# A gated linear-recurrence layer and its feed-forward block: the last block's sums and stores in two halves, and the clamps of the gate logits moved ahead in the schedule

## The chip, the core and the metric

The kernel runs on one core of a Trainium2 chip. The core has a matrix engine (PE, which also loads its weights: PEld), a vector engine (DVE), a scalar engine (ACT, which evaluates functions by tables), a general engine (POOL) and a sequencer for transfers (SP). Each engine takes its own instructions strictly in order and waits for the others through semaphores. DMA transfers are issued by SP or by ACT and run beside the engines. The metric is the device time of one execution in microseconds; lower is better.

## The reference

Two stages. The first keeps a 48x48 state for each of 4x8 heads over 768 steps; the second is a feed-forward block with an unusual activation.

```python
f = 1.0 / (1.0 + np.exp(-f_logit))                      # q, k, v, f_logit: (4, 8, 768, 48)
for t in range(S):
    state = f[:, :, t, :, None] * state + np.einsum('bhd,bhe->bhde', k[:, :, t], v[:, :, t])
    y[:, :, t] = np.einsum('bhd,bhde->bhe', q[:, :, t], state)
x = y.transpose(0, 2, 1, 3).reshape(3072, 384)
h = x @ w_in                                            # (384, 2048)
g = h * erf(np.maximum(h, 0.0) + np.log1p(np.exp(-np.abs(h))))
out = g @ w_out                                         # (2048, 384)
```

## The kernel before

The 3072 rows of `x` are cut into 24 chunks of 128 rows, two to a block: 12 blocks of 256 rows. A chunk `g` passes through four stages. `stage_d` (L374) multiplies the prepared gate logits by a triangle on PE (L380), and ACT and DVE make decayed copies of q and k from it (L383, L386, L395, L399). `stage_t` (L403) transposes them on PE and copies the results from PSUM: `qA` by two ACT instructions (L418), `kT` by ACT or, from chunk 9, by DVE (L422). `stage_s` (L443) makes the scores and updates the state (DVE L438, L439); `stage_y` (L504) makes `y` on PE (L525), and ACT copies it into `xT` (L529). The PSUM tiles of `stage_d`, `stage_t` and `stage_y` come in turn from one pool of two buffers, `ps_at`, so `stage_y` has to wait until `stage_t`'s copies have freed one.

Before `stage_d`, `prepare` (L357) turns a whole block's logits into log(1+exp(-x)): a clamp on DVE (L360, 128x768 elements, in place), then Exp and Ln on ACT (L364, L365, in place), with a table load ahead of them if ACT last used the other set of functions (L347).

The second stage per block: `hidden` (L578) makes four groups of 1024 columns on PE (L587), each copied by ACT from PSUM (L594). `activate` (L539) then works on a group in steps: Exp on ACT (L157), two Tanh on ACT (L160), two multiplications on DVE (L165), Tanh on ACT (L559), a last multiplication on DVE (L561); two groups overlap, so that one step of one group's L561 goes with the next group's second L165. `project_first` (L659, blocks 0 and 1) is the plain product with `w_out`; `project` (L687, blocks 2 to 11) uses seven half-size products instead of eight, whose factors come from sums on DVE (L615). Its parts are added up by DVE in `plus` (L726) into five row pieces `rows_sb` (a slice of the tile `scratch`), and `store` (L652) sends four of them to the output in one transfer on SP (384 KB, L654).

The order of the work is written by hand. Iteration `it` walks through a list of slots, each a step of the second stage (`slots`, L761: a slot of `hidden` is one product of 128x256, of `project` one of 128x192; the profile counts two matmul instructions for each, as the data are 32-bit). After a slot `s` the loop (L930 to L985) puts in, in this order: rounding steps of the weights, a stage of the recurrence if `s` is in the list `at`, loads of logits, `prepare` of block `it + 3` at `prepare_at` (14 slots ahead of the `stage_d` that needs it, L928), an activation step (`act_step`, in iteration 2 where `s % 5` is 1 or 3), and a step of sums. All engines' queues follow from this one order. In iteration 2 the stages stand at slots 3, 11, 19, 28 (d9, s8, t9, y8 for chunks 9 and 8) and on, and `prepare_at` is 22.

In the last block `project` computes products 1, 2, 6, then 5, 7, then 3 and 4 in turn; 3 and 4 share a PSUM tile of pool `ps_sc`. After the last product DVE does one sum of two pieces (128x384) and one of a single piece (128x192), then SP stores all 256 rows. What follows in every engine's program is a conditional jump: the kernel holds a second, general version for extreme gates (`general`, L991), and `flag` (L1168, L1169) says whether it is needed. Each engine loads the flag, jumps over the general code and signs off; SP waits for every DMA's semaphore first.

Of the kernel before, what the change touches and what calls it, by code (L numbers as in the profile page):

```python
# [43 lines left out]
FP32 = mybir.dt.float32  # L44
# [26 lines left out]
P = 128  # L71
# [3 lines left out]
def kernel(  # L75
# [10 lines left out]
    nc = tc.nc  # L86
# [10 lines left out]
    CPB = 2  # L97
    TB = CPB * P
    n_blocks = B * S // TB
# [118 lines left out]
    lts = {}  # L218
# [124 lines left out]
    def use_exp_ln():  # L343
        if sets[0] == EXP_LN:
            return
        sets[0] = EXP_LN
        nc.scalar.add_instruction(  # L347
            mybir.InstLoadActFuncSet(
                act_func_set_id=EXP_LN, name=nc.get_next_instruction_name(),
                engine=mybir.EngineType.Activation, ins=[], outs=[],  # L350
            )
        )
# [1 line left out]
    def other_set():  # L354
        sets[0] = 0

    def prepare(blk, j0, j1):  # L357

        lt = lts[blk][:, j0:j1, :].rearrange("t j c -> t (j c)")
        nc.vector.tensor_scalar(  # L360
            out=lt, in0=lt, scalar1=LOGIT_MIN, scalar2=None, op0=ALU.max
        )
        use_exp_ln()
        nc.scalar.activation(out=lt, in_=lt, func=AF.Exp, scale=-1.0)  # L364
        nc.scalar.activation(out=lt, in_=lt, func=AF.Ln, bias=1.0)  # L365

    busy = []

# [283 lines left out]
    def store(blk):  # L652
# [3 lines left out]
            in_=rows_sb[:, 0:4, :].rearrange("p (t two) c -> p t (two c)", t=CPB),  # L656
        )

    def project_first(blk):  # L659

        ops = ps_moe.tile([P, 2, 512], FP32, name="ops", tag="moe")
        for gi in range(n_g):
            gr = groups[blk, gi]
            for tt in range(CPB):
                for j in range(FG):
                    ft = gi * FG + j
                    assert n_pieces + ft * n_pieces // n_ft in rounded
                    while not gr["done"]:
                        act_step()
                    nc.tensor.matmul(  # L670
                        ops[:, tt, 0:d_model],
                        lhsT=gr["h"][:, j, tt * P : (tt + 1) * P],
                        rhs=w_out_sb[:, ft, :],
                        start=(ft == 0), stop=(ft == n_ft - 1),
                    )
                    if j == FG - 1 and tt == CPB - 1:
                        if blk == 0:
                            to_sum.append(sum_w(gi))
                        if gi == n_g - 1:
                            nc.scalar.copy(  # L680
                                out=rows_sb[:, 0:4, :].rearrange("p (t two) c -> p t (two c)", t=CPB),
                                in_=ops[:, :, 0:d_model],
                            )
                            store(blk)
                    yield

    def project(blk):  # L687


        ops = [ps_moe.tile([P, 2, 512], FP32, name="ops", tag="moe") for _ in range(2)]  # L690
        end = blk == n_blocks - 1
        ops.append(ps_sc.tile([P, 2, 512], FP32, name="ops", tag="sc") if end else ops[1])
        place = {n: ops[i][:, j, k * DH : (k + 1) * DH] for n, (i, j, k) in {
            1: (0, 0, 0), 2: (0, 1, 0), 6: (0, 1, 1), 5: (1, 0, 0), 7: (1, 0, 1), 3: (2, 1, 0), 4: (2, 1, 1),
        }.items()}
        first = [1, 2, 5, 3]

        def pair(n):
            i, j = {2: (0, 1), 5: (1, 0), 3: (2, 1)}[n]
            return ops[i][:, j, 0 : 2 * DH].rearrange("p (n c) -> p n c", n=2)  # L700

        def products(gis, ns):
            for gi in gis:
                gr = groups[blk, gi]
                while gr["sums"] is None:
                    sum_step()
                a11, a12, a21, a22 = blocks(gr["h"])
                w = w_out_sb[:, FG * gi : FG * (gi + 1), :]
                s, t = gr["sums"], w_sums(gi)
                for j in range(2):  # L710
                    w1, w2 = w[:, j, :], w[:, 2 + j, :]
                    for n in ns:
                        x, y = {
                            1: (a11, w1[:, 0:DH]), 2: (a12, w2[:, 0:DH]), 3: (s[2], w2[:, DH:]),
                            4: (a22, t[:, 3, j, :]), 5: (s[0], t[:, 0, j, :]),
                            6: (s[1], t[:, 1, j, :]), 7: (a21, t[:, 2, j, :]),
                        }[n]
                        nc.tensor.matmul(  # L718
                            place[n], lhsT=x[:, j, :], rhs=y,
                            start=(gi == 0 and j == 0 and n in first),  # L720
                            stop=(gi == n_g - 1 and j == 1), skip_group_check=True,
                        )
                        yield

        def plus(out, x, y):
            nc.vector.tensor_tensor(out=out, in0=x, in1=y, op=ALU.add)  # L726

        o = rows_sb
        yield from products((0, 1), (1, 2, 6))
        yield from products((0,), (5, 7, 3, 4))  # L730
        to_sum.appendleft(sum_h(groups[blk, 3]))
        yield from products((1,), (5, 7, 3, 4))
        yield from products((2, 3), (1, 2, 6))
        nc.scalar.copy(out=o[:, 3, :], in_=place[1])  # L734

        plus(o[:, 0:5:4, :], o[:, 3:4, :].broadcast_to((P, 2, DH)), pair(2))
        def fives():

            plus(o[:, 3:5, :], o[:, 4:5, :].broadcast_to((P, 2, DH)), pair(5))

        yield from products((2, 3), (5, 7))
        if end:

            fives()
        yield from products((2, 3), (3, 4))
        if not end:
            fives()
        plus(o[:, 1:3, :], o[:, 3:5, :], pair(3))
        plus(o[:, 3, :], o[:, 3, :], place[7])
        store(blk)  # L750
# [42 lines left out]
    with tc.manual_schedule():  # L793
# [119 lines left out]
        for it in range(n_blocks):  # L913
# [16 lines left out]
            for s, _ in enumerate(gen):  # L930
                due += (1 if s < 42 else 0.6 if s < 72 else 0.3) if it == 0 else 0.42 if it == 1 else 0.6
                while due >= 1:
                    weights_step()
                    due -= 1
                if s % 6 == 3:
                    load_more()
                if at and s == at[0]:
                    at.popleft()
                    f, g = todo.popleft()
                    f(g)  # L940
                    if f in (stage_y, stage_y_s):
                        if g + NSV < n_chunks:
                            load_sv(g + NSV)
                        load_to(g + LOOK)
                        if g == 2:
                            load(5, "v")
                            load_piece(7)
                if it == 0 and s == 14:
                    prepare(2, 0, CPB)
                if it == 0 and s == 9:  # L950
                    load_f(6)
                    load_f(7)
                if s == n // 2 and it + 4 < n_blocks:
                    for j in range(CPB):
                        load_f((it + 4) * CPB + j)
                if it + 3 < n_blocks and s == prepare_at:
                    prepare(it + 3, 0, CPB)
                if it < 2:
                    step = it == 1 and s % 6 == 3
                elif it == 2:  # L960
                    step = s % 5 in (1, 3)
                elif it == 3:
                    step = s % 7 in (1, 4)
                elif it == n_blocks - 1:
                    step = s % 3 == 1
                else:
                    step = s % 9 in (2, 6)
                if step:
                    act_step()
                if it == 2:  # L970
                    if s % 2:
                        sum_step()
                elif it > 2:
                    if s == n - n_h and it < n_blocks - 1:
                        to_sum.extend(sum_h(groups[it - 1, gi]) for gi in range(NS))
                    if it == n_blocks - 1 and s % n_o == 40 and s < 2 * n_o:
                        blk = n_blocks - 2 + s // n_o
                        to_sum.extend(sum_h(groups[blk, gi]) for gi in range(NS))
                    if it == 3:
                        if s % 2:  # L980
                            sum_step()
                    elif s < n_o or s % 3 == 0 or it == n_blocks - 1:
                        sum_step()
                if it == n_blocks - 2 and s in (5, 40):
                    next(check)  # L985
# [215 lines left out]
```

## Time and profile before

| what | value |
|---|---|
| median of 6 runs | 619.54 us (618.51 to 621.52) |
| profiled execution, its own time | 619.03 us |
| its span, first to last instruction | 617.3 us |
| mean granted PE clock | 0.981 |
| busy: PE / PEld | 588.4 us (95%) / 515.0 us (83%) |
| busy: DVE / ACT / POOL | 460.3 us (75%) / 382.4 us (62%) / 15.4 us (2%) |
| clamp on DVE (L360, 128x768), x10 of 14 | 0.55 us median |
| Exp and Ln on ACT (L364, L365) | 0.84 us each, median |
| ACT's waits for the clamp (L364 for L360) | 16.0 us in 8 waits, longest 5.0 |
| store of a block (384 KB), issue to landing, x12 | 2.4 / 2.6 / 4.5 us (min / median / max) |

The span leaves out 1.7 us of the profiled execution's own time. Busy shares are means over phases with different limits: PE is close to saturated from about 80 us on, while the weights are still being rounded on DVE and ACT in the first quarter.

### The profile page before, as it was taken

The page shows a single profiled execution, that of the slowest core. Times are in us where ns is not written, and L with a number is a line of the kernel's source. Part 1 is how long each engine was busy: PE and PEld are TensorE (multiplying, and loading weights), DVE is VectorE, ACT ScalarE, POOL GpSimd, SP SyncE. Part 2 cuts the span into 40 slices and gives each one's busy share as a digit, 9 for nine tenths or more (in the row PEclk, how much of TensorE's full clock was granted, in tenths as well). Part 3 has the DMA queues.
Part 4 walks back from the last instruction along what each step waited for, and adds up shares of the span by engine and source line. Part 5 has one row for each costly group of instructions (what it writes and reads, how often), then busy time and mean ns, then how long its engine had stood idle before and what let it go on. Part 6 is the DMA issues. An engine that isn't in the chain of part 4 may idle for free.

```text
span 617.3 us, 13765 instructions
## 1 busy us (share of the span) xinstructions
PE 588.4 (95%) x5729; PEld 515.0 (83%) x5729; DVE 460.3 (75%) x784; ACT 382.4 (62%) x483; POOL 15.4 (2%) x33
## 2 busy tenths in 40 slices
PE   8789699999999999999999999999999999999995
PEld 7568587887655689989989989989989989989995
DVE  4898998697499597897796776896886785647551
ACT  5735347987875778775866675875766566366000
POOL 1000011010000000000000000000000000000000
PEclk9878899999999999999999999999999999999998
DMA  9997743450231223223133222132121000000000
GB/s 204 258 236 213 213 136 63 70 101 7 50 78 27 52 52 52 48 57 54 33 71 53 40 65 53 33 72 53 29 52 14 3 27 0 28 1 0 27 27 29
DMA packets 155587, 41.35 MB, mean 67 GB/s; under 512 B 147328, under 2 KB 150400, under 8 KB 155520
## 3 DMA queue, kind: packets, MB, share of 16 engines
q1 hardware_dynamic: 153440, 40.02, 29.5%
q8 instruction: 47, 0.77, 0.5%
q10 hardware_dynamic: 2080, 0.39, 0.3%
q14 instruction: 20, 0.16, 0.1%
HBM read 35.59 MB, written 4.72 MB: 65 GB/s over the span
## 4 chain that ended last, share of the span: by engine, by line
PE 72%; DVE 14%; ACT 7%; issue 3%; DMA 2%; SPq 1%; POOL 0%; DVEq 0%; ACTq 0%; POOLq 0%
PE hps L587 29%; PE ops L718 25%; PE ops L670 7%; PE y L525 3%; PE ps_t L411 3%; PE ps_d L380 2%; ACT x L160 2%; DVE sv L438 1%; PE sc L468 1%; PE sc L460 1%; DVE sv L439 1%; DVE w_in_sb L322 1%; DVE w_in_sb L336 1%; DVE Hg L561 1%; DVE w_out_sb L331 1%
## 5 line engine op out<-in xcount | busy, mean ns | idle before, releaser
L587 PE MATMUL hps<-xT,w_in_sb 128*128 128x256 f32 x1152 | 265.7, 387 | 6.6 <-DVE w_in_sb L336 4.4
L587 PEld LDWEIGHTS hps<-xT,w_in_sb 128*128 128x128 f32 x1152 | 219.0, 193 | 40.3 <-DVE w_in_sb L336 3.4
L165 DVE SCALAR_TENSOR_TENSOR e<-x,e 128x1024 f32<-128x1024 f32 x96 | 117.1, 1220 | 13.1 <-ACT x L160 12.6
L160 ACT ACTIVATE x<-Hg,serf_bias 128x1024 f32<-128x1024 f32 x88 | 97.5, 1140 | 0.2
L157 ACT ACTIVATE e<-Hg 128x1024 f32<-128x1024 f32 x44 | 46.5, 1058 | 61.8 <-DVE Hg L561 57.7
L718 PE MATMUL ops<-wT,Hg 128*128 128x192 f32 x320 | 78.9, 328 | 0.0
L561 DVE TENSOR_TENSOR Hg<-Hg,e 128x1024 f32<-128x1024 f32 x44 | 53.8, 1222 | 22.2 <-ACT e L559 21.9
L718 PE MATMUL ops<-wT,scratch 128*128 128x192 f32 x288 | 67.8, 326 | 0.9 <-DVE scratch L726 0.9
L718 PE MATMUL ops<-w_out_sb,Hg 128*128 128x192 f32 x320 | 65.1, 326 | 0.0
L594 ACT COPY Hg<-hps 128x1024 f32<-128x1024 f32 x44 | 44.4, 1009 | 32.8 <-PE hps L587 32.4
L718 PEld LDWEIGHTS ops<-wT,Hg 128*128 128x128 f32 x320 | 55.8, 190 | 1.9
L718 PEld LDWEIGHTS ops<-w_out_sb,Hg 128*128 128x128 f32 x320 | 54.6, 190 | 2.0
L559 ACT ACTIVATE e<-e 128x1024 f32<-128x1024 f32 x48 | 50.3, 1049 | 1.9 <-DVE e L165 1.8
L718 PEld LDWEIGHTS ops<-wT,scratch 128*128 128x128 f32 x288 | 50.2, 190 | 1.1 <-issue 1.1
L496 DVE TENSOR_TENSOR qA<-sc,tri 64x256 f32<-64x256 f32 x68 | 28.7, 422 | 24.6 <-PE sc L468 23.6
L726 DVE TENSOR_TENSOR scratch<-scratch,ops 128x384 f32<-128x384 f32 (+1 forms) x40 | 20.1, 503 | 31.8 <-ACT scratch L734 24.5
L418 ACT COPY qA<-ps_t 64x512 f32<-64x512 f32 x48 | 27.7, 577 | 24.4 <-PE ps_t L411 22.4
L395 DVE TENSOR_TENSOR qd<-qn,dp 128x384 f32<-128x384 f32 x24 | 13.4, 557 | 32.7 <-ACT dp L383 32.6
L525 PEld LDWEIGHTS y<-qA,sv 128*32 128x32 f32 x1536 | 23.7, 110 | 14.1 <-issue 11.3
L718 PE MATMUL ops<-w_out_sb,scratch 128*128 128x192 f32 x144 | 35.2, 326 | 0.0
L438 DVE TENSOR_TENSOR sv<-sc,sv 48x192 f32<-48x192 f32 x80 | 28.4, 355 | 8.3 <-ACT qA L488 6.9
L525 PE MATMUL y<-qA,sv 128*32 128x64 f32 x1536 | 27.8, 221 | 6.0 <-issue 4.6
(111 smaller groups left out, 651.4 us busy)
## 6 DMA issues: line engine op xcount, KB each, us to landing
lt<-in_f_logit_dram SPq DMA_DIRECT2D x24, 192.0 KB, 3.7
qn<-in_q_dram SPq DMA_DIRECT2D x24, 192.0 KB, 3.2
out_dram<-scratch SPq DMA_DIRECT2D x12, 384.0 KB, 2.6
kn<-in_k_dram SPq DMA_DIRECT2D x23, 192.0 KB, 3.5
vt<-in_v_dram SPq DMA_DIRECT2D x23, 192.0 KB, 3.6
sv<-in_v_dram SPq DMA_DIRECT2D x84, 48.0 KB, 2.8
w_out_sb<-in_moe_w_in_dram SPq DMA_DIRECT2D x4, 768.0 KB, 6.0
Hg<-in_moe_w_in_dram SPq DMA_DIRECT2D x4, 768.0 KB, 6.1
```

The lines of the kernel that those rows point to most:

```text
L157: nc.scalar.activation(out=dst[:], in_=h, func=AF.Exp)
L160: nc.scalar.activation(out=dst[:], in_=h, func=AF.Tanh, bias=serf_bias[:, i : i + 1], scale=SERF_KAB[i][0])
L165: nc.vector.scalar_tensor_tensor(out=e[:], in0=x[:], scalar=SERF_KAB[i][2], in1=e[:], op0=ALU.add, op1=ALU.mult)
L438: nc.vector.tensor_tensor(out=new, in0=add, in1=old, op=ALU.add)
L496: nc.vector.tensor_tensor(out=qA[half(1 - r), r, :, half(c)], in0=sc[half(c), r], in1=tri1[half(c)].unsqueeze(1).broadcast_to((C, HP, C)), ...
L525: nc.tensor.matmul(y[M * i : M * (i + 1), kt, half(c)], lhsT=sv[:, r, c, a, o : o + M], rhs=qA[:, r, a, half(c)], start=(n == 0), stop=Tru ...
L559: nc.scalar.activation(out=e[:], in_=e[:], func=AF.Tanh, scale=SERF_C)
L561: nc.vector.tensor_tensor(out=h, in0=h, in1=e[:], op=ALU.mult)
L587: nc.tensor.matmul(hps[:, j, :], lhsT=w_in_sb[:, kt, ft * P : (ft + 1) * P], rhs=xTs[blk][:, kt, :], start=(kt == 0), stop=(kt == n_k - 1),)
L594: nc.scalar.copy(out=gr["h"], in_=hps[:])
L670: nc.tensor.matmul(ops[:, tt, 0:d_model], lhsT=gr["h"][:, j, tt * P : (tt + 1) * P], rhs=w_out_sb[:, ft, :], start=(ft == 0), stop=(ft == ...
L718: nc.tensor.matmul(place[n], lhsT=x[:, j, :], rhs=y, start=(gi == 0 and j == 0 and n in first), stop=(gi == n_g - 1 and j == 1), skip_grou ...
```

## The change

Two independent edits. In the last block, products 3 and 4 no longer alternate: all of 3 is done first, and 4 gets a PSUM tile of its own. After product 3 the first 128 rows are summed and stored on SP; the last sum of one piece follows product 4, and the other 128 rows are stored on ACT's queue. And `prepare` in the loop is split: the clamp is put in six slots ahead of Exp and Ln (iterations 0 to 8; the calls of `prepare` ahead of the loop and for block 2 stay as they were).

```diff
-    def prepare(blk, j0, j1):
-
+    def clamp(blk, j0, j1):
         lt = lts[blk][:, j0:j1, :].rearrange("t j c -> t (j c)")
         nc.vector.tensor_scalar(
             out=lt, in0=lt, scalar1=LOGIT_MIN, scalar2=None, op0=ALU.max
         )
+
+    def logs(blk, j0, j1):
+
+        lt = lts[blk][:, j0:j1, :].rearrange("t j c -> t (j c)")
         use_exp_ln()
         nc.scalar.activation(out=lt, in_=lt, func=AF.Exp, scale=-1.0)
         nc.scalar.activation(out=lt, in_=lt, func=AF.Ln, bias=1.0)
+
+    def prepare(*which):
+        clamp(*which)
+        logs(*which)
...
+    def store_tile(blk, t, queue):
+        r = blk * TB + t * P
+        queue.dma_start(
+            out=out[r : r + P, :],
+            in_=rows_sb[:, 2 * t : 2 * t + 2, :].rearrange("p two c -> p (two c)"),
+        )
...
         first = [1, 2, 5, 3]
+        if end:
+            place[4] = ps_at.tile([P, 512], FP32, name="ops4", tag="at")[:, 0:DH]
+            first.append(4)
...
         if end:
 
             fives()
+            yield from products((2, 3), (3,))
+            plus(o[:, 1, :], o[:, 3, :], place[3])
+            store_tile(blk, 0, nc.sync)
+            plus(o[:, 3, :], o[:, 3, :], place[7])
+            yield from products((2, 3), (4,))
+            plus(o[:, 2, :], o[:, 4, :], place[4])
+            store_tile(blk, 1, nc.scalar)
+            return
         yield from products((2, 3), (3, 4))
-        if not end:
-            fives()
+        fives()
         plus(o[:, 1:3, :], o[:, 3:5, :], pair(3))
         plus(o[:, 3, :], o[:, 3, :], place[7])
         store(blk)
...
+                if it + 3 < n_blocks and s == prepare_at - 6:
+                    clamp(it + 3, 0, CPB)
                 if it + 3 < n_blocks and s == prepare_at:
-                    prepare(it + 3, 0, CPB)
+                    logs(it + 3, 0, CPB)
```

## The prediction

> **What bounds the kernel now.** I read the page first, for how full PE is, then the waits, then two windows of the timeline (the tail and the stretch around the moved clamps), then the rows of single lines.
>
> ```profile
> PE   8789699999999999999999999999999999999995
> DVE  4898998697499597897796776896886785647551
> ```
>
> From the sixth slice (77 us) on PE is full in every slice but the last. So an edit counts only if it moves one of PE's few remaining waits or the tail. Counted from the trace, PE's waits of 0.2 us or more after 80 us are: 0.26 us at 93.05, 0.41 at 116.6, 0.88 at 151.0, 0.63 at 156.2, 0.42 at 163.9, 1.5 at 175.6, 1.0 at 360.3 and 0.88 at 577.9.
>
> The tail, in the timeline and in the rows of three lines:
>
> ```profile
> 610.63 0.94 DVE L726 TENSOR_TENSOR scratch<-scratch,ops 128x384 f32<-128x384 f32 x2 [2.04 <-PE ops L718]
> 611.60 0.37 SPq L654 DMA_DIRECT2D out_dram<-scratch  x1
> ...
> DMA to landing us min/median/max: 4.1/4.1/4.1
> ...
> L1168 DVEq TENSOR_LOAD <-flag x1: 542/542/542, 611.2 to 611.2; - x1
> ...
> L1169 DVEq COMPARE_BRANCH  x1: 72/72/72, 611.9 to 611.9; - x1
> L1169 DVEq EVENT_SEMAPHORE  x1: 21/21/21, 615.7 to 615.7; - x1
> ```
>
> Two chains start at the last sums and end together. The store is issued at 611.60 and lands 4.13 us later, at 615.73. DVE loads the flag as its last sum starts (611.22), jumps at 611.85 and runs its next instruction only at 615.70: 3.77 us, in which one 16 KB instruction packet moves (612.49 to 613.95). SP then works off its closing row from 615.74 to 616.37, the barrier of all engines takes the rest to 617.3. The sixth of SP's eight closing steps waits for DVE, so DVE alone would let SP finish at about 615.97.
>
> **The tail, step by step.** The number of products stays, so PE's last one still ends at 610.60. Product 3 is done four slots earlier, 4 x 0.325 = 1.30 us, at 609.29. Its sum (0.35 us, the row of the 128x192 sum), SP's issue at about 609.72 and the sum with product 7 (0.35) all lie beside PE's last four slots; the first store is down by 609.72 + 2.4 to 4.5 (the twelve stores' bounds), at most 614.3, and ends nothing. After the last product only one 128x192 sum is left where there were a 128x384 and a 128x192: DVE's last sum starts at 610.63 instead of 611.22, its flag, jump and next instruction follow 0.59 us earlier, at 615.11, and SP could finish 0.25 us after that, at 615.38 instead of 616.37: **-0.99 us** if the store lets it.
>
> ACT issues the second store at 610.63 + 0.35 + 0.03 = 611.01. ACT has had nothing to do since 605.8; behind this issue on its queue stand only the flag load (0.47 us) and a jump that took it 0.18 us, so ACT is ready by 612.2. The trace has no 192 KB store. From one side, whole stores that met no instruction packet land after 2.4 us: 613.4, with which DVE decides (-0.99). From the other, the slowest store took 4.54: 615.55. I take the row nearest to it, the last store: it began 0.88 us after issue, together with DVE's instruction packet, and the queue that shares a DMA engine with that packet finished after it, 17 packets of 0.068 us. The jump and the issue move together, so they meet again: packet until 613.35, then 9 packets, 0.6 us, then 0.46 us to the semaphore as before: 614.4. The semaphores go round, and the one after the last store's is the first that SP waits for; seven more waits (0.53 us) and the closing row (0.63) follow, 615.6. So the tail is worth **-0.77 us**, with bounds of -0.99 and, for a landing at 615.55, +0.35.
>
> The Trainium skill (DMA: Bandwidth & Descriptors, Rules for kernel authors) speaks against this split: spreading transfers over SP and ACT buys no bandwidth, since both run on the same sixteen DMA engines, and only issue time is saved. [...] The same skill (Runtime: NRT & Kernel Launch, Instruction fetch mechanics) says that a taken jump out of the loaded pages waits for a fetch; the 3.77 us of DVE's row are what the sum goes by.
>
> **The clamps, block by block.** The work is the same; the order on DVE changes, and ACT's waits for it.
>
> ```profile
> ACT lt L364 <- DVE lt L360: 16.0, 8, 5.0
> ```
>
> Four of the eight waits belong to the calls ahead of the loop and one (1.67 us) to block 2, all untouched. Three are touched: 5.03 us (block 3), 1.50 (block 6, at 205.5) and 0.57 (block 11, at 442.4).
>
> Block 3, iteration 0:
>
> ```profile
> 85.67 0.59 ACT L420 COPY kT<-ps_t 128x512 f32<-128x512 f32 x1
> 91.28 0.84 ACT L364 ACTIVATE lt<-lt 128x768 f32<-128x768 f32 x1 [5.03 <-DVE lt L360]
> 92.16 0.84 ACT L365 ACTIVATE lt<-lt 128x768 f32<-128x768 f32 x1
> ...
> L380 PE MATMUL ps_d<-lt,tri x2: 486/538/590, 93.1 to 93.5; 128*128 128x384 f32 x2
> ```
>
> DVE is six slots behind with rounding. Six slots earlier in its queue the clamp stands ahead of two rounding steps, four state updates and a third rounding step: at about 87.0 instead of 90.7. Exp then starts 3.7 us earlier, and the product of `stage_d` at 93.05, which waited 0.26 us for Ln, waits no more: **-0.26 us**. The rest of ACT's 3.7 us is nobody's wait: PE was fed in between. DVE gains 0.72 us of idle at 93.8, where it waited for ACT's next rounding step; it loses it again in the 2.06 us that it waits for PE's `stage_d` at 108.2.
>
> Block 5, iteration 2, slot 16 instead of 22:
>
> ```profile
> 146.25 1.23 DVE L165 SCALAR_TENSOR_TENSOR e<-x,e 128x1024 f32<-128x1024 f32 x1
> 147.40 1.22 DVE L561 TENSOR_TENSOR wT<-wT,e 128x1024 f32<-128x1024 f32 x1
> ...
> 152.01 0.56 DVE L360 TENSOR_SCALAR lt<-lt 128x768 f32<-128x768 f32 x1
> ...
> 148.65 1.06 ACT L157 ACTIVATE e<-wT 128x1024 f32<-128x1024 f32 x1 [1.98 <-DVE wT L561]
> 149.72 1.17 ACT L418 COPY qA<-ps_t 64x512 f32<-64x512 f32 x2
> ...
> 150.99 1.35 PE L525 MATMUL y<-qA,sv 128*32 128x64 f32 x64 [0.88 <-issue]
> ```
>
> Slot 13's activation step issues the first of these DVE rows, slot 16's the second; the clamp of slot 16 goes between them, as a stage or clamp is put in ahead of its slot's activation step. DVE has no gap from 144.70 to 152.49, so L561 ends 0.48 us later (152.01 to 152.49, the clamp's spacing). ACT had been waiting for it 1.98 us; its Exp, the two copies behind it and PE's `y`, which waits for the second copy (semaphore at 150.89), all move by 0.48. The chain goes on without slack: ACT is busy from there to L594 at 155.1 (PE waits at 156.2), L559 and L561 at 159.6, L594 at 162.8 (PE waits at 163.9), and by L561 at 166.6 and the scores to PE's wait at 175.6. Nothing there takes the delay up: **+0.48 us**. Here Exp did not wait for the clamp but for its own table load (152.08 to 153.36), so nothing is earned.
>
> The others I cost at nothing, with this cover. Block 4: the clamp falls into DVE's idle 1.67 us ahead of 112.0, and Exp waits for a table load. Block 6: ACT is 1.50 us earlier, but PE has no wait from 176 to 360; without that cover it would be -1.50. Blocks 7 to 11: a clamp moved ahead of the first sum of a block may push that sum by up to 0.48, and PE first needs its PSUM tile about 7 us later (300.7 against 307.8 for block 8). The logits of all nine have been down for 18 us or more at the new place (block 5: 128.7 against 147.4), so no clamp blocks DVE for a transfer.
>
> **Sum**: 619.03 - 0.77 - 0.26 + 0.48 = 618.48, that is -0.55 us. The median of the runs shown is 619.54, 0.51 above the profiled run; I shift it by the same amount: **619.0 us**, no change by the 0.2% (1.24 us) that a measurement of this kernel can tell.
>
> **Rivals.**
> *Clamps pay.* If iteration 2's clamp is off the chain (block 5 costs nothing) and DVE's 0.72 us of block 3 reach PE's waits at 151 to 176, the sum is -0.99 - 0.26 - 0.72 = -1.97: 617.6. For it: all five PE waits from 116 to 176 hang on ACT and DVE. Against: DVE's idle 2.06, 1.67 and 2.58 us between 106 and 121 swallow such a gain. Chance 0.22.
> *The split store earns nothing.* A landing at 615.55 gives +0.35 in the tail, with the clamps +0.57: 620.1. For it: the store at 577.7, which also met one instruction packet, took 4.5 us. Against: half the packets. Chance 0.20.
> *Slower: the second sum waits for the first store.* The sum with product 7 writes `rows_sb` while the first store reads it. If the order by semaphores holds for the whole tile `scratch`, that sum waits for a landing, 609.72 + 2.4 to 4.5 = 612.1 to 614.2; the last sum starts 0.35 later instead of at 611.22, DVE's jump follows, and SP ends at that start + 4.48 + 0.27: 617.2 to 619.3, +0.9 to +2.9, with the clamps +1.1 to +3.1: about 621.6. It costs from a landing 1.5 us after issue on. Against: DVE wrote other parts of `scratch` at 408.9 while the store of 407.95 was on its way until 410.5. Chance 0.08.
>
> **How the numbers follow.** The forecast has 0.50. The six runs shown spread over 3 us, so a median can be off by some 0.5. Range 617.7 to 620.3: from the clamps' rival to past the late store; the slower rival is left out. Faster by over 0.2% (under 618.3): most of the first rival and a tenth of the forecast, 0.27. Slower (over 620.8): the last rival and a rest, 0.10. Within: 0.63.
>
> **What would show it.** In the tail: a single 128x192 sum after the last product, DVE's instruction after the jump 0.6 us earlier against that product, the second store down before it. At block 3: ACT's 5.03 us wait down to about 1.4, no wait of `stage_d`. At block 5: the clamp directly ahead of L561, and PE's `y` wait grown from 0.88 to about 1.36. I am wrong if the clamp stands elsewhere there, if ACT's jump now misses its page (3.7 us on, as on PE and DVE), or if any PE wait is new after 176 us.

## The result, and the profile after

The changed kernel takes 618.28 us (median of 21 runs, 616.27 to 620.21) against 619.32 us for the kernel before (46 runs): a ratio of 0.9982, 95% interval 0.9975 to 0.9989. That is 1.0 us less, from 0.7 to 1.5. The forecast was 0.55 us less.

The profiled execution of the changed kernel is a lucky one: 616.41 us, span 614.7. It was ahead of the profiled execution before from the beginning, at a higher granted clock, as the first 75 us of the two show (columns: stretch, its length, busy time of PE, PEld, DVE, ACT and POOL with the number of instructions, PE's granted clock, DMA share, GB/s). Before:

```profile
0.00:75.00 75.00, 58.61 (x732) 48.72 (x733) 62.25 (x118) 37.89 (x69) 3.51 (x15) 0.86 0.90 223
```

After:

```profile
0.00:75.00 75.00, 57.62 (x740) 46.85 (x741) 62.63 (x119) 38.69 (x70) 3.53 (x15) 0.91 0.91 222
```

At 0.91 instead of 0.86 PE has done eight matmul instructions more by then. The clock alone does not explain it: the trace of `clamps_alone`, below, has 0.91 there too and only two more. Set against each other instruction by instruction, PE is 1.74 us ahead at 75 us, ahead of any part of the change. So the two spans, 2.5 us apart, must not be subtracted. What can be compared is the tail, counted from the start of PE's last matmul instruction, and single PE waits.

The tail of the changed kernel, in its timeline:

```profile
609.57 0.35 DVE L743 TENSOR_TENSOR scratch<-scratch,ops 128x192 f32<-128x192 f32 x1 [0.56 <-PE ops L735]
609.95 0.37 ACTq L668 DMA_DIRECT2D out_dram<-scratch  x1
```

In the rows of the store's line, ACT's part, and of DVE's flag load and jump (L1194, L1195 in this kernel):

```profile
DMA to landing us min/median/max: 2.3/2.3/2.3
```

```profile
L1194 DVEq TENSOR_LOAD <-flag x1: 540/540/540, 609.6 to 609.6; - x1
```

```profile
L1195 DVEq COMPARE_BRANCH  x1: 72/72/72, 610.2 to 610.2; - x1
L1195 DVEq EVENT_SEMAPHORE  x1: 21/21/21, 613.7 to 613.7; - x1
```

PE's last matmul starts at 609.20 here. One narrow sum is left after it, the second store is down at 612.21, 2.25 us after its issue, and DVE's instruction after the jump follows at 613.69, 1.5 us behind the store: DVE's jump, not the store, now ends the work. From PE's last matmul to the end of the span it is 5.51 us instead of 6.99: 1.48 us less.

The clamp of block 5 on DVE, and PE's wait behind it:

```profile
144.71 1.23 DVE L165 SCALAR_TENSOR_TENSOR e<-x,e 128x1024 f32<-128x1024 f32 x1
145.86 0.55 DVE L359 TENSOR_SCALAR lt<-lt 128x768 f32<-128x768 f32 x1
146.33 1.22 DVE L568 TENSOR_TENSOR wT<-wT,e 128x1024 f32<-128x1024 f32 x1
```

```profile
149.92 1.21 PE L532 MATMUL y<-qA,sv 128*32 128x64 f32 x64 [1.39 <-issue]
```

The clamp (L359) stands directly ahead of L568 (L561 before), without a gap, and PE's wait ahead of `y` is 1.39 us instead of 0.88.

Block 3, on ACT, and `stage_d`'s product on PE:

```profile
83.93 0.59 ACT L427 COPY kT<-ps_t 128x512 f32<-128x512 f32 x1
87.35 0.84 ACT L367 ACTIVATE lt<-lt 128x768 f32<-128x768 f32 x1 [2.84 <-DVE lt L359]
```

```profile
L387 PE MATMUL ps_d<-lt,tri x2: 486/486/486, 91.0 to 91.4; 128*128 128x384 f32 x2
its engine sat idle before it (us, times) until:
who waited for it (us, times):
```

ACT's wait fell from 5.03 to 2.84 us, and PE no longer waits for Ln: nothing stands under "sat idle before it".

### The profile page after: what moved, and what is told of

Read it like the earlier page. It is cut to its first block, busy times and chain, and to the rows that moved or that the text cites. A ratio compares the mean times of both kernels' runs of the same rounds, so it can differ in the third digit from the quotient of the medians.

```text
span 614.7 us, 13769 instructions
## 1 busy us (share of the span) xinstructions
PE 585.6 (95%) x5729; PEld 511.6 (83%) x5729; DVE 461.3 (75%) x785; ACT 382.7 (62%) x483; POOL 14.7 (2%) x33
## 4 chain that ended last, share of the span: by engine, by line
PE 70%; DVE 15%; ACT 7%; DMA 4%; issue 2%; SPq 1%; DVEq 0%; ACTq 0%
PE hps L594 28%; PE ops L735 26%; PE ops L684 7%; PE y L532 3%; PE ps_t L418 2%; DMA qn<-in_q_dram 2%; ACT x L160 2%; PE ps_d L387 2%; PE sc L467 1%; PE sc L475 1%; DVE sv L445 1%; DVE w_in_sb L322 1%; DVE sv L446 1%; DMA Hg<-in_moe_w_out_dram 1%; DVE w_in_sb L336 1%
## 5 line engine op out<-in xcount | busy, mean ns | idle before, releaser
L568 DVE TENSOR_TENSOR Hg<-Hg,e 128x1024 f32<-128x1024 f32 x44 | 53.8, 1222 | 22.6 <-ACT e L566 22.4
L532 PE MATMUL y<-qA,sv 128*32 128x64 f32 x1536 | 29.4, 224 | 12.4 <-issue 5.1
```

What stands on the lines that cost most here:

```text
L532: nc.tensor.matmul(y[M * i : M * (i + 1), kt, half(c)], lhsT=sv[:, r, c, a, o : o + M], rhs=qA[:, r, a, half(c)], start=(n == 0), stop=Tru ...
L568: nc.vector.tensor_tensor(out=h, in0=h, in1=e[:], op=ALU.mult)
```

## The experiments

Theory A: the new tail brings all of the gain, and the clamps cost net 0.2 us (-0.26 at block 3, +0.48 at block 5). Theory B: the clamps bring part of it. All ratios are to the kernel before, timed on the same chip beside it.

**tail_alone**, the changed kernel with the clamps at their old slots.

```diff
-                if it + 3 < n_blocks and s == prepare_at - 6:
-                    clamp(it + 3, 0, CPB)
                 if it + 3 < n_blocks and s == prepare_at:
-                    logs(it + 3, 0, CPB)
+                    prepare(it + 3, 0, CPB)
```

> The changed kernel with the clamps back at their old slots, so only the last block's new tail. Theory A (the tail brings all of the gain, the clamps cost net 0.24 us): from the start of PE's last product to the end of the span 5.5 us as in the changed kernel, against 7.0 before; 1.3 to 1.5 us under the kernel before in the median (ratio 0.9976 to 0.9979); PE's wait ahead of y at 151 us stays at 0.88 us, and stage_d at 93 us keeps its 0.26. Theory B (the moved clamps bring part of the gain): at most 0.5 us under the kernel before.

Measured: 617.95 us against 619.57, ratio 0.9976 (0.9968 to 0.9985), 1.5 us less. Tail 5.40 us, PE's wait at 151 us 0.85. Counted from start to start, PE loses 0.18 us to Ln at 93 us (0.26 in the kernel before), so a little less than expected stays there. By the medians the tail alone earns no less than the whole change.

**clamps_alone**, the kernel before with the nine clamps moved.

```diff
+                if it + 3 < n_blocks and s == prepare_at - 6:
+                    clamp(it + 3, 0, CPB)
                 if it + 3 < n_blocks and s == prepare_at:
-                    prepare(it + 3, 0, CPB)
+                    logs(it + 3, 0, CPB)
```

> The kernel before with nothing but the nine clamps moved six slots ahead. Theory A: ACT's wait for block 3's clamp falls from 5.0 us to under 3, PE's wait for Ln at stage_d (0.26 us at 93 us) is gone, PE's wait ahead of y at 151 us grows from 0.88 to 1.36 us, no other PE wait after 176 us changes; the tail stays at 7.0 us; net +0.2 us, ratio 1.0003, not to be told from no change. Theory B: 0.5 us or more under the kernel before, with shorter PE waits between 110 and 176 us.

Measured: 619.72 us against 619.57, ratio 1.000 (0.9989 to 1.0011). Tail 6.85 us. ACT's wait for block 3's clamp is 0.97 us. No wait of PE at 93 us; at 151 us it is longer:

```profile
150.70 1.21 PE L532 MATMUL y<-qA,sv 128*32 128x64 f32 x64 [1.34 <-issue]
```

PE's other waits from 110 us on are those of the kernel before within 0.15 us (0.41, 0.77, 0.42, 1.51, 1.00, 0.87). Theory B falls: no wait between 110 and 176 us got shorter. The expected +0.2 us is less than the times can tell; the two waits show it.

**block5_back**, the changed kernel with only block 5's clamp at its old slot.

```diff
-                if it + 3 < n_blocks and s == prepare_at - 6:
+                if it + 3 < n_blocks and s == prepare_at - (0 if it == 2 else 6):
```

> The changed kernel, but the clamp of block 5 (iteration 2) back at its old slot, the other eight six slots ahead. Theory A: DVE runs L165, L568, L165 there without the clamp in between, PE's wait ahead of y at 150 us is 0.88 instead of 1.39 us, and the time is 0.48 us under the changed kernel, 1.5 us under the kernel before (ratio 0.9975). Rival: the wait of 1.39 us comes from the run's own start (PE was 1.1 us ahead of the traced run before), not from the clamp; then it stays above 1.2 us and the time equals the changed kernel's.

Measured: 617.58 us against 619.57, ratio 0.9971 (0.996 to 0.9982).

```profile
151.07 1.21 PE L532 MATMUL y<-qA,sv 128*32 128x64 f32 x64 [0.88 <-issue]
```

The wait is back at 0.88, so it came from the clamp and not from the beginning of the run.

**five_slots**, all nine clamps five slots ahead.

```diff
-                if it + 3 < n_blocks and s == prepare_at - 6:
+                if it + 3 < n_blocks and s == prepare_at - 5:
```

> The changed kernel with all nine clamps five slots ahead instead of six. In iteration 2 the clamp then comes behind slot 16's activation step. Theory A (the cost is the one place ahead of L568): DVE runs L165, L568, L165, then the clamp; PE's wait ahead of y at 151 us is 0.88 us, stage_d at 93 us has no wait for Ln; the time is that of block5_back, 0.4 to 0.5 us under the changed kernel, ratio 0.997 to 0.9975. Rival (any clamp ahead of its old place delays DVE's chain there): the wait stays near 1.35 us.

Measured: 617.56 us against 619.70, ratio 0.996 (0.9946 to 0.9975). DVE and PE:

```profile
146.44 1.23 DVE L165 SCALAR_TENSOR_TENSOR e<-x,e 128x1024 f32<-128x1024 f32 x1
147.58 1.22 DVE L568 TENSOR_TENSOR wT<-wT,e 128x1024 f32<-128x1024 f32 x1
148.72 1.22 DVE L165 SCALAR_TENSOR_TENSOR e<-x,e 128x1024 f32<-128x1024 f32 x1
149.85 0.55 DVE L359 TENSOR_SCALAR lt<-lt 128x768 f32<-128x768 f32 x1
```

```profile
151.17 1.21 PE L532 MATMUL y<-qA,sv 128*32 128x64 f32 x64 [0.86 <-issue]
```

One slot later the clamp is behind the activation step and costs PE nothing. It is not the clamp's being early that costs, but what it is put in front of. All eleven profiles divide cleanly: the four kernels with this clamp six slots ahead wait 1.33 to 1.39 us there, the seven with it elsewhere (the kernel before among them) 0.84 to 0.91.

**one_store**, the sums in the changed kernel's order, but one store of all rows after the last.

```diff
             plus(o[:, 1, :], o[:, 3, :], place[3])
-            store_tile(blk, 0, nc.sync)
             plus(o[:, 3, :], o[:, 3, :], place[7])
             yield from products((2, 3), (4,))
             plus(o[:, 2, :], o[:, 4, :], place[4])
-            store_tile(blk, 1, nc.scalar)
+            store(blk)
             return
```

> The changed kernel with its sums ordered as there, but one store of all 256 rows on SP after the last sum in place of two. Theory A (DVE's jump after the last sum sets the end, the sums' order earns it): issue 0.4 us after the last product, DVE's next instruction after the jump within 0.4 us of where the changed kernel has it (4.5 us after the last product's start); if the store lands after 2.5 us the tail is as in the changed kernel, 5.5 us, if it meets DVE's instruction packet again and lands after 4.1 us, 6.2 us. Rival (the split store earns the gain): the tail goes back to 6.7 us or more.

Measured: 618.57 us against 619.57, ratio 0.9987 (0.9978 to 0.9995). Tail 5.99 us, between the two cases of A: the order of the sums alone brings 1.0 of the 1.48 us, the split another 0.5. The store lands 3.60 us after issue, and DVE's next instruction comes 3.84 us after its jump, as before (3.85), where the split has 3.50.

**before_no_jump** and **after_no_jump**, the two kernels without the general version, the flag load and the jump over it.

```diff
-    bad = nc.values_load(flag[0:1, 0:1], min_val=0, max_val=1)
-    with tc.If(bad > 0):
-        general()
```

> The kernel before without the general version and without the flag load and jump over it (left out: the fall-back for extreme gates, which these inputs never take). Theory A: with no instruction packet in its way the store lands 2.5 us after issue, SP follows; tail 5.2 us instead of 7.0, ratio 0.997. Rival (the jump is hidden behind the store): tail 6.9 us or more, ratio 1.

> The changed kernel without the general version, the flag load and the jump (the same part left out). Theory A: the new tail then earns only the earlier issue and the smaller second store, 0.3 to 0.8 us: tail 4.4 to 4.9 us against 5.2 of before_no_jump. Rival (two half stores earn the gain by themselves): the tail is 1.4 us or more under that of before_no_jump, as with the jump.

Measured: 617.01 and 616.33 us against 619.70, ratios 0.9958 (0.9944 to 0.9972) and 0.9943 (0.9925 to 0.9961). The tails are 4.60 and 3.58 us. The store of before_no_jump:

```profile
L654 SPq DMA_DIRECT2D out_dram<-scratch x1: 373/373/373, 611.1 to 611.1; - x1
...
DMA to landing us min/median/max: 2.4/2.4/2.4
```

The same 384 KB lands 2.4 us after issue where it took 4.1 with the jump. No 16 KB instruction packet moves in this tail; the one that moves beside the store in the kernel before held it up by 1.7 us (the last section says whose packet it is). Both tails are shorter than expected, as a second row of closing waits on SP goes with the jump. And without the jump the change earns 1.01 us of tail, more than theory A's 0.3 to 0.8 and less than the rival's 1.4: the store is issued 0.58 us earlier and, being half, lands 0.53 us sooner after its issue (1.90 against 2.44); SP's closing takes the remaining 0.10 back. So with no jump the split would pay by itself; with the jump DVE decides.

**act_last**, block5_back with the last sum off DVE: a product with the identity adds the piece to product 4's tile, and ACT copies it out.

```diff
+            nc.tensor.matmul(
+                place[4], lhsT=ident[:], rhs=o[:, 4, :], start=False, stop=False, skip_group_check=True
+            )
             yield from products((2, 3), (4,))
-            plus(o[:, 2, :], o[:, 4, :], place[4])
+            nc.scalar.copy(out=o[:, 2, :], in_=place[4])
```

> block5_back with the last sum off DVE: product 4's PSUM tile first takes the piece o[4] by a product with the identity (two more matmul instructions, 0.33 us of PE), and ACT copies the finished piece out instead of DVE's sum. Theory A (DVE's jump sets the end): DVE's last sum is then the one with product 7, its jump is over about 3.3 us after PE's last product starts, the store (issued 0.7, landed 3.0) ends last, SP signs off 1.2 us behind it at 4.1 to 4.2 instead of 4.72; tail 4.9 instead of 5.47, less 0.33 us on PE: net 0.2 to 0.3 us under block5_back, ratio 0.9965 to 0.997. Rival (the store sets the end already): tail 5.4 to 5.5 and the time 0.3 us over block5_back.

Measured: 617.24 us against 619.70, ratio 0.9961 (0.9946 to 0.9976). Tail 5.06 instead of 5.47, with DVE's instruction after the jump 2.78 us after PE's last matmul starts, ahead of the store's landing at 3.14. DVE's rows, and the DMA packets that begin between the two (from 610.18 to 613.19 us: queue and kind, packets, MB, share of the 16 DMA engines):

```profile
L1198 DVEq COMPARE_BRANCH  x1: 72/72/72, 610.2 to 610.2; - x1
L1198 DVEq EVENT_SEMAPHORE  x1: 21/21/21, 613.2 to 613.2; - x1
```

```profile
q1 hardware_dynamic: 144, 0.20, 19.6%
q10 hardware_dynamic: 144, 0.20, 18.1%
q14 instruction: 2, 0.02, 2.3%
```

With DVE's jump out of the way the end moved, which confirms that it was the bound. The two added matmul instructions (0.33 us) take back most of the 0.40 us; in time it is not to be told from five_slots.

**stores_on_sp**, five_slots with both stores issued by SP.

```diff
-            store_tile(blk, 1, nc.scalar)
+            store_tile(blk, 1, nc.sync)
```

> five_slots with both half stores issued by SP. Theory A (ACT's queue has no part in the gain): the second store is issued at the same 0.75 us after PE's last product starts, its first packets follow 0.88 us later, it lands 2.0 to 2.5 us after issue; DVE's jump still ends the tail at 5.4 to 5.6 us; the time is that of five_slots, ratio 0.996 to 0.9975. Rival (a queue of its own lets the second store past the first, or past DVE's instruction packet): on SP it lands 3.4 us or more after issue and the tail is 6.0 us or more.

Measured: 617.70 us against 619.43, ratio 0.9965 (0.9953 to 0.9977). The second store is issued at the same place and lands 2.21 us later; the tail is 5.32 us, a little under the 5.4 to 5.6 expected, as DVE's next instruction comes 3.17 us after its jump. ACT's queue has no part in the gain. The Trainium skill (DMA: Bandwidth & Descriptors, Rules for kernel authors) says that spreading transfers over SP and ACT buys nothing but issue time; this run agrees, with 2.21 us on SP against 2.21 to 2.27 on ACT in the four kernels with this tail, the jump and the store on ACT.

## Why the prediction came out as it did

The direction was right, and so were the two steps of the clamps. The tail was sized at half of what it is: the forecast had the second store ending it, and DVE's jump does.

- **Tail, forecast -0.77 us, measured -1.48.** The step that failed is the second store's landing: I took 3.4 us after issue, and it was 2.25. I had read the 16 KB packet as that of DVE's jump, which moves together with the store's issue, so that the two would meet again. The packet is PE's (last section), and PE's jump did not move: from the start of PE's last matmul the packet begins at 2.22 us before and at 2.20 after, while the store's first packets went from 2.22 to 1.63. So SP was not held by the store, and the bound by DVE that I had given (-0.99) applied. Two smaller terms I had not seen: DVE's instruction came 3.50 instead of 3.85 us after its jump begins, and the closing barrier took 0.14 us less, as ACT's last step in it took 0.01 instead of 0.14 us and no longer came last. The sum by the traces: 0.59 (last sum starts earlier, as forecast) + 0.35 (jump) + 0.40 (SP no longer waits for the store's landing) + 0.14 = 1.48.
- **Block 3, forecast -0.26: right.** The clamp ran at 86.8 us (forecast 87.0), and PE's wait for Ln is gone in all eight kernels with the move. Without it PE loses, from start to start, 0.26 us (before), 0.18 (tail_alone) and nothing (before_no_jump) ahead of `stage_d`'s first matmul instruction, and about 0.1 us more in each between the first and the second, so there is 0.1 to 0.4 us to earn, by the execution. ACT's remaining wait is 2.84 us and not 1.4 because PE, and ACT with it, was ahead of DVE in that execution; in the other seven it is 1.14 us or less.
- **Block 5, forecast +0.48: right**, in place, cause and size (0.84 to 0.91 against 1.33 to 1.39 us, and undone by one slot).
- **The other clamps, forecast 0: right.** From 156 to 578 us PE's waits are the same in all eleven profiles within 0.15 us. A wait of 0.22 us at 98.4 us in the changed kernel's trace stands in none of the other seven with the move.
- **Sum.** -1.48 - 0.26 + 0.48 = -1.26 by the traces; the medians say -1.0 (0.7 to 1.5). The forecast of -0.55 lies outside that interval. It was called no change by the bound of 0.2%; the result, 0.18%, lies within that bound, and with the many runs it is told from no change all the same.
- **Rivals.** *Clamps pay*: clamps_alone shows none of it. *The split store earns nothing*: it rested on a late landing, which did not come; the split earns 0.5 us (one_store). *The second sum waits for the first store*: DVE started it at 608.66, 0.01 us after that store's issue, and the store landed at 610.67. ACT's jump stayed short: its next instruction came 0.19 us after.

That the range held the time is in part luck. The measured 618.28 lies 0.7 us under the forecast (0.2 of it because the kernel before, too, came out at 619.32 in many runs and not at 619.54), and the range reached so far down for a rival that the runs refute, the clamps that pay; the best tail that the forecast allowed (-0.99) leads only to 618.8.

## What to carry to other kernels

Before shortening the last transfer, read every engine's last instructions: a jump over code that is never run cost this kernel 2.6 us at its end (ratio 0.9958 without it). In the traces the tail is 2.4 us shorter without it (6.99 to 4.60): 1.7 us because the store is no longer held up by an instruction packet, the rest in SP's closing. When an instruction is moved ahead in a hand-written order, look at what it is put directly in front of on its own engine; here one slot decided between a cost of 0.5 us and none. The best versions here, the new tail with the clamps five slots ahead or block 5's left alone, take 2.0 to 2.1 us off the kernel before (act_last 2.5, not to be told from them).

## What the runs showed of the hardware

Instruction packets and data hold each other up on the DMA engines, and whichever comes first there makes the other wait. All times here are counted from the start of PE's last matmul instruction.

Before, a 16 KB packet (queue q8) and the store's first packets both start at 2.22 us; the packet takes 1.46 us, and the store's last data packets go until 4.99, against 3.42 without the jump. Of the 16 signals that make up the store's landing 13 are in by 3.77 us and the last at 5.46. In the changed kernel the store's packets are first (1.63 to 2.39), and the 16 KB packet starts at 2.20 and takes 0.88. In one_store the store's packets start at 1.63 too and go until 2.95; the 16 KB packet starts only then, at 2.95, and the store's last signal comes at 4.35, 0.49 us after the end of that packet.

The prediction called this packet DVE's. It is PE's, by three signs in the traces. In act_last none of these packets begins between DVE's jump and its next instruction, as the view above shows: q8 is not among the queues; the packet before started ahead of the jump, and the last one starts 0.60 us after that instruction. There are 47 of them in the whole run, and from 300 to 600 us of the kernel before every two follow 464 to 537 instructions of PE, weight loads counted, and 31 to 60 of DVE. And the last one follows PE's jump: it starts 0.5 to 0.9 us after PE goes on behind its jump in all eight kernels with the jump other than one_store, where the store's packets were ahead of it; in act_last, where PE goes on 1.0 to 1.4 us later than in the others, it starts at 3.38 instead of 2.20 to 2.41. So it does not move when the store's issue does, and issuing the store 0.58 us earlier takes the store out of its way. That is worth more than the size of the store: 1.7 us against 0.5 (2.44 to 1.90 without the jump).

DVE's jump fits the 8 KB packets on queue q14. Before, two of them start at 3.53 and 3.57 us, after the jumps of DVE (1.58) and SP (1.76), as most of the store's packets have run out; in the changed kernel SP jumps earlier, and the packet that follows DVE's jump (0.99) starts at 2.40, again as the store's packets end (2.39). DVE goes on 1.4 to 1.8 us after the end of its packet in all nine kernels with the jump. By this reading the smaller, earlier store lets DVE's packet start 1.40 instead of 1.95 us after its jump, and the 0.35 us that DVE gained there are what is left of that. No run tests it: the traces do not name the engine that a packet is for, nor its DMA engine.
